# Half-unit operand places, reordered cosine steps and six sum places in a fused attention and two-MLP kernel

## The chip, the cores and the metric

The kernel runs on one core of one Trainium2 chip, in one launch. The metric is the device time of that launch in microseconds. The core's engines are named as in the profile: PE multiplies matrices (PEld is its weight load), DVE is the vector engine, ACT the scalar engine, POOL the third elementwise engine, and SP is the queue that issues every DMA of this kernel.

## The reference

Attention over mean-pooled keys, then two MLPs over the 4608 x 512 result, all in float32:

```python
x = attention(q, k pooled by 8, v pooled by 8)        # (4608, 512)
gate = sigmoid(x @ w_gate)                            # w_gate, w_val: (512, 1536)
x = (gate * (x @ w_val)) @ w_out                      # w_out: (1536, 512)
h = x @ w_in                                          # w_in: (512, 2048)
out = (h * cos(h)) @ w_out2                           # w_out2: (2048, 512)
```

## The kernel before, in words

Every matrix operand is held as two float32r parts, a high part (a rounded copy, made by ACT) and a low part (what is left of it, made by DVE in `split_lo`, line 65); three matmuls, high by high, high by low and low by high, make one product. The large products use a seven-product scheme on quarter blocks (as Strassen's), so sums of blocks are made on POOL. All intermediate results go through DRAM. Tokens are taken in nine chunks of 512; `GROUPS` are chunk 0 alone and four pairs of chunks.

The launch runs in four stages, each ending before the next begins on PE:

- **Gate and value** (`gv_step`, `gated`): attention, `w_gate` and `w_val` for all chunks. The gated results go to DRAM (`od`).
- **Units of `w_out`** (line 817 on): for each of the four pairs, seven products of three units each, 84 units. A unit is 12 matmuls of 128x512, 6 for each of its two halves. `unit_fetch` (848) loads a unit of 512 KB from `od` into one of three raw places `uf`; `unit_high` (841) makes the high part with one ACT cast of 128x1024 into one of two `up` places; `unit_low` (836) makes the low part with one DVE subtraction. A `up` place can be written again only when PE has finished the unit in it. `unit_go` (860) does one such step of each kind and is called about once per unit, so casts are issued at most two units ahead of the matmuls. When a product is done (`product_done`, 924), its two PSUM banks are copied by ACT (line 930) or added by DVE (line 940) into one of the `ok` tiles in pool `hm`, which has five places `x0` to `x4`; POOL makes sums of these tiles (`x_sum`, line 910), and SP stores them to `xd` (line 907). Between units the same engines prepare `w_in`: SP loads 16 raw blocks of 512 KB (`i2_begin`, 274), ACT and DVE convert them, and `i2_fill` (322) splits 28 weights. What happens at which unit is written by hand: `at_(n, f)` (898) puts `f` at the n-th following call of `due` (901), which is called once per unit.
- **Cosine blocks** (`Block`, `h_block`, line 1055): h and h cos h for five groups of eight blocks. A block has seven products of 6 matmuls each, in the order 0, 3, (product 6 of the block before), 2, 1, 5, 4, in PSUM banks A to D, of which there are two sets. `kept` (1007) copies a bank, `whole` (1011) rounds to an integer on ACT, `rest` (1015) takes the fraction on DVE, `sine` (1022) is on ACT and `times` (1026) on DVE; line 1061 copies bank A to C, lines 1080 and 1088 add a bank to a kept tile. POOL makes four sums per block (1042). `after(pos)` follows each product and calls `due`; operands `x` of the next group are loaded (955), cast (960) and split (65) from there. In group 0 matmuls have 256 columns, in groups 1 to 4 they have 512.
- **Second output product** (`y_chunk`): operands `sp` come back from DRAM (1141), are cast (1152) and split, and 28 weights `wy` of 512 KB take the places of the weights of the cosine stage during its last group.

Within an engine all instructions run in the order in which the program issues them; there is no scheduler.

Of the kernel before, what the change touches and what calls it, by code (L numbers as in the profile page):

```python
# [9 lines left out]
F32 = mybir.dt.float32  # L10
# [12 lines left out]
def attention_two_mlps(  # L23
# [794 lines left out]
    count = {"fetched": 0, "high": 0, "low": 0, "done": 0, "go": 0}  # L818
    o_weights, o_tags, o_raw, o_parts = [], [], {}, {}
# [13 lines left out]
    uf = []  # L833
    issued = {}

    def unit_low():
        x, raw = o_parts[count["low"]], o_raw.pop(count["low"])
        split_lo(nc.vector, x[:, 1], raw, x[:, 0])
        count["low"] += 1

    def unit_high():
        k = count["high"]
        x = xq.tile([P, 2, 2, C], F32R, tag=f"q{3 + k % 2}", name=f"up{k}")
        nc.scalar.copy(x[:, 0], o_raw[k])  # L844
        o_parts[k] = x
        count["high"] += 1

    def unit_fetch():
        k = count["fetched"]
        g, n, m = units[k]  # L850
        pool, tag = uf[k % 3]
        t = pool.tile([P, 2, C], F32, tag=tag, name=f"uf{k}")
        nc.sync.dma_start(
            t.rearrange("p m (i n) -> p m i n", i=2), od[g][O_PRODUCTS[n][1], :, 2 * m:2 * m + 2]
        )
        o_raw[k] = t
        issued[k] = count["go"]
        count["fetched"] += 1

    def unit_go():  # L860

        if count["low"] < count["high"]:
            unit_low()
        count["go"] += 1
        if count["high"] < min(count["done"] + 2, count["fetched"]):
            if count["go"] - issued[count["high"]] >= 2:
                unit_high()
        if count["fetched"] < min(count["low"] + len(uf), len(units)):
            unit_fetch()

    def unit_step():

        k = count["done"]
        g, n, m2 = units[k]
        while count["low"] <= k:
            unit_go()
        which, fresh = O_PRODUCTS[n][2:]
        if n < 2 and m2 == 0:
            po[g, which] = [bank("tg"[g % 2 == 0], [P, C], f"po{g}_{which}{u}") for u in range(2)]
        w = o_weights[k % PER]  # L880
        x = o_parts.pop(k)
        for m in range(2):
            first, final = fresh and m2 == 0 and m == 0, m2 == STEPS - 1 and m == 1
# [7 lines left out]
        if m2 == STEPS - 1:  # L891
            product_done(g, n, po[g, which])
# [663 lines left out]
```

## Time and profile before

| quantity | value |
|---|---|
| time, median of 3 runs | 1885.22 us (1883.74 to 1885.65) |
| the profiled execution | 1891.42 us, its span 1889.7 us |
| busy PE, DVE, ACT, POOL | 1753.8, 1103.1, 896.3, 629.7 us |
| DMA | 401.77 MB, mean 213 GB/s |
| gate and value, units of `w_out` | 0 to 778.6 us, 778.6 to 1124.8 us |
| cosine blocks, second output product | 1124.8 to 1529.3 us, 1529.3 to 1889.7 us |

The stage bounds are the first matmuls of lines 887, 991 and 1229 (lines 626 to 628 and 789 to 791 come before). Busy PE counts overlapping matmuls by modelled ends, so within a stage its gaps say more than its sum.

### The profile page before, as it was taken

The numbers are of one execution on the slowest core, as the hardware profiler recorded it, in microseconds if no ns is written. First come the engines' busy times: TensorE is split into PE (matmuls) and PEld (weight loads), VectorE is DVE, ScalarE is ACT, GpSimd is POOL, SyncE is SP. The second block draws the span as 40 slices with busy tenths as digits, with TensorE's granted clock in tenths as the row PEclk, the third lists the DMA queues.
The fourth block names the chain that finished last, engine by engine and source line by source line (L and its number), as shares of the span: only waits on it lengthen the run. The fifth ranks groups of instructions, "written<-read, shape, count | busy, mean of one in ns | idle before, by whom it ended". The sixth has DMA issues, their size and how long they took to land. (4 is left out here: it accounts for less than half of the span.)

```text
span 1889.7 us, 26169 instructions
## 1 busy us (share of the span) xinstructions
PE 1753.8 (93%) x9360; PEld 1430.4 (76%) x9360; DVE 1103.1 (58%) x1734; ACT 896.3 (47%) x1513; POOL 629.7 (33%) x622
## 2 busy tenths in 40 slices
PE   7999999999999999886778768999999989999999
PEld 5887888888888888665556557777777778888887
DVE  7956565475654621264535555676767666655565
ACT  7555445354544521243434435565666544444443
POOL 2314546345453332223322024465656430000000
PEclk8999999999999999997989989999999999999999
DMA  9635757657666479576556635485768997676663
GB/s 274 183 101 159 212 167 238 190 173 210 217 206 223 154 274 307 191 251 213 187 182 204 213 142 173 157 266 174 245 195 265 343 345 260 224 228 205 224 202 127
DMA packets 266418, 401.77 MB, mean 213 GB/s; under 512 B 54448, under 2 KB 197808, under 8 KB 266288
## 3 DMA queue, kind: packets, MB, share of 16 engines
q1 hardware_dynamic: 266288, 400.10, 65.6%
q8 instruction: 73, 1.20, 0.3%
q14 instruction: 57, 0.47, 0.1%
HBM read 226.75 MB, written 173.28 MB: 212 GB/s over the span
## 5 line engine op out<-in xcount | busy, mean ns | idle before, releaser
L640 DVE TENSOR_TENSOR g<-pv,g 128x512 f32<-128x512 f32 (+1 forms) x111 | 74.9, 675 | 299.0 <-issue 148.4
L65 DVE TENSOR_TENSOR sp<-sp,sp 128x1024 fp32r<-128x1024 f32 x126 | 154.0, 1262 | 97.5 <-ACT sp L1152 97.4
L626 PE MATMUL pg<-xT,wg 128*128 128x512 f32 (+1 forms) x444 | 179.3, 404 | 3.9 <-ACT e L551 3.0
L628 PE MATMUL pg<-xT,wg 128*128 128x512 f32 (+1 forms) x444 | 172.5, 389 | 2.2 <-DVE wg L65 2.2
L627 PE MATMUL pg<-xT,wg 128*128 128x512 f32 (+1 forms) x444 | 172.2, 388 | 0.8 <-DVE xT L65 0.8
L626 PE MATMUL pv<-xT,wv 128*128 128x512 f32 (+1 forms) x444 | 170.9, 385 | 2.1 <-DVE g L640 2.1
L628 PE MATMUL pv<-xT,wv 128*128 128x512 f32 (+1 forms) x444 | 170.9, 385 | 0.0
L627 PE MATMUL pv<-xT,wv 128*128 128x512 f32 (+1 forms) x444 | 170.8, 385 | 0.0
L65 DVE TENSOR_TENSOR up<-uf,up 128x1024 fp32r<-128x1024 f32 x84 | 119.5, 1434 | 75.3 <-ACT up L844 75.0
L844 ACT CAST up<-uf 128x1024 fp32r<-128x1024 f32 x84 | 88.1, 1050 | 150.4 <-PE po_A L889 66.4
L1042 POOL TENSOR_TENSOR s_S<-z_a,z_a 128x512 f32<-128x512 f32 (+1 forms) x80 | 100.3, 1276 | 170.7 <-DVE z_a L1026 170.7
L991 PE MATMUL pha<-x,hw 128*128 128x512 f32 (+1 forms) x320 | 129.1, 403 | 24.3 <-DVE ph L1088 13.4
L639 ACT ACTIVATE g<-pg 128x512 f32<-128x512 f32 (+1 forms) x111 | 65.0, 587 | 153.6 <-PE pg L628 92.5
L1229 PE MATMUL py_A<-wy,sp 128*128 128x512 f32 x432 | 135.7, 395 | 0.0
L1152 ACT CAST sp<-sp 128x1024 fp32r<-128x1024 f32 x126 | 124.3, 1058 | 12.5 <-DMA sp<-sd 12.5
L995 PE MATMUL pha<-x,hw 128*128 128x512 f32 (+1 forms) x320 | 120.2, 376 | 0.0
L996 PE MATMUL pha<-x,hw 128*128 128x512 f32 (+1 forms) x320 | 120.1, 375 | 0.0
L888 PE MATMUL po_A<-up,so 128*128 128x512 f32 x192 | 83.5, 435 | 37.5 <-DVE up L65 37.5
L1022 ACT ACTIVATE z_a<-z_a 128x512 f32<-128x512 f32 (+1 forms) x160 | 93.8, 587 | 45.3 <-DVE z_a L1015 45.3
L991 PEld LDWEIGHTS pha<-x,hw 128*128 128x128 f32 x320 | 61.2, 191 | 60.8 <-DVE ph L1088 24.7
L628 PEld LDWEIGHTS pg<-xT,wg 128*128 128x128 f32 x444 | 84.4, 190 | 20.1 <-DVE wg L65 2.4
L626 PEld LDWEIGHTS pg<-xT,wg 128*128 128x128 f32 x444 | 84.7, 191 | 19.6 <-ACT e L551 3.2
(193 smaller groups left out, 4449.1 us busy)
## 6 DMA issues: line engine op xcount, KB each, us to landing
sp<-sd SPq DMA_DIRECT2D x126, 512.0 KB
uf<-od SPq DMA_DIRECT2D x84, 512.0 KB
sd<-s_S SPq DMA_DIRECT2D x128, 256.0 KB
od<-tg SPq DMA_DIRECT2D x48, 512.0 KB
sd<-z_a SPq DMA_DIRECT2D x96, 256.0 KB
wo<-wo SPq DMA_DIRECT2D x40, 512.0 KB
raw_o<-in_moe_w_out_dram SPq DMA_DIRECT2D x28, 512.0 KB
x<-xd SPq DMA_DIRECT2D x28, 512.0 KB
```

Of the source, the lines that this page charges most:

```text
L65: engine.tensor_tensor(out=lo, in0=x, in1=hi.bitcast(F32), op=ALU.subtract)
L626: nc.tensor.matmul(p, wh, x[:, 0, kb], start=kb == 0, stop=False)
L627: nc.tensor.matmul(p, wh, x[:, 1, kb], start=False, stop=False)
L628: nc.tensor.matmul(p, wl, x[:, 0, kb], start=False, stop=kb == KB - 1)
L844: nc.scalar.copy(x[:, 0], o_raw[k])
L991: nc.tensor.matmul(p, wh, x[:, 0, kb], start=k in (0, 3) and kb == 0, stop=False, skip_group_check=True,)
L995: nc.tensor.matmul(p, wh, x[:, 1, kb], start=False, stop=False, skip_group_check=True)
L996: nc.tensor.matmul(p, wl, x[:, 0, kb], start=False, stop=kb == 1, skip_group_check=True)
L1022: nc.scalar.activation(z, z, AF.Sin, scale=TURN)
L1042: nc.gpsimd.tensor_tensor(out=z[name], in0=z[x], in1=z[y], op=op)
L1152: nc.scalar.copy(hi[:, r], lo[:, r].bitcast(F32))
L1229: nc.tensor.matmul(p, x[0][:, m, s], w, start=fresh and m == 0, stop=False, skip_group_check=True,)
```

## The change

Three things are rewritten.

1. **Units of `w_out` become 168 halves** of 6 matmuls each. There are four tiles of two places each, eight places, allocated once (`up`). A half of 256 KB is loaded straight into the low part of its place, ACT casts it into the high part, and DVE subtracts in place. The raw places `uf` are gone. After the matmuls of half v the program issues the split of half v+3, the cast of half v+4 and the load of half v+8. The first eight loads, six casts and four splits are issued in the last steps of the stage before.
2. **Sums get six places** (`a` to `f`), and a table `HOMES` says which result of which pair goes where; three stores of sums are issued one unit earlier. The `w_in` raw blocks use other places, and `i2_fill` of the last pair comes one unit earlier.
3. **Cosine steps are issued in another order** within a block, directly and not through `at_`: the previous block's last steps (`a`) stand between the present block's (`b`). Casts of `x` are all on ACT, and POOL splits one operand of a group where it split three. The first operands and the weights of the last stage are issued from a table of positions (`put`), the first operand's split in two parts in two blocks.

```diff
-    def unit_high():
-        k = count["high"]
-        x = xq.tile([P, 2, 2, C], F32R, tag=f"q{3 + k % 2}", name=f"up{k}")
-        nc.scalar.copy(x[:, 0], o_raw[k])
...
+    def up_of(v):
+        return up[v // 2 % len(up)][:, v % 2]
+
+    def half_fetch(upto):
+        while count["fetched"] < min(upto + 1, len(halves_of)):
+            v = count["fetched"]
+            g, n, m = halves_of[v]
+            nc.sync.dma_start(
+                up_of(v)[:, 1].bitcast(F32).rearrange("p (i n) -> p i n", i=2),
+                od[g][O_PRODUCTS[n][1], :, m],
+            )
+            count["fetched"] += 1
...
+    def half_step(v):
...
+        half_low(v + 3)
+        half_high(v + 4)
+        half_fetch(v + 2 * len(up))
+        if final:
             product_done(g, n, po[g, which])
...
+    HOMES = {
+        (1, 0): "a", (1, 1): "e", (1, 2): "c", (1, "S2"): "d", (1, 6): "b",
+        (2, 0): "e", (2, 1): "c", (2, 2): "a", (2, "S2"): "b", (2, 6): "d",
+        (3, 0): "c", (3, 1): "a", (3, 2): "e", (3, "S2"): "d", (3, 6): "f",
+        (4, 0): "a", (4, 1): "e", (4, 2): "b", (4, "S2"): "c", (4, 6): "d",
+    }
...
-            t = hm.tile([P, 2, C], F32, tag=f"x{n if n < 6 else 3}", name=f"ok{g}_{n}")
-            o_keep[n] = t
+            t = o_keep[n] = home(g, n)
...
+        if b:
+            b.product(5)
+        if a:
+            a.sums()
+        if b:
+            b.sine("a11")
+            nc.vector.tensor_tensor(out=b.p["B"], in0=b.p["B"], in1=b.z["a12"], op=ALU.add)
+            b.times("a11", "C")
+            b.whole("a12", "B")
         after(5)
-        step(4)
-        nc.vector.tensor_tensor(out=b.p["D"], in0=b.p["A"], in1=b.z["a22"], op=ALU.add)
-        b.whole("a22", "D")
-        at_(1, lambda: b.rest("a22", "D"))
-        at_(1, lambda: b.sine("a22"))
-        at_(2, lambda: b.times("a22", "D"))
-        at_(3, lambda: b.store("a22"))
+        if b:
+            b.product(4)
+            nc.vector.tensor_tensor(out=b.p["D"], in0=b.p["A"], in1=b.z["a22"], op=ALU.add)
+            b.rest("a12", "B")
+            b.whole("a22", "D")
+            b.store("a11")
         after(6)
...
-        for k in range(len(units)):
-            unit_step()
-            unit_go()
-            due()
+        for v in range(len(halves_of)):
+            half_step(v)
+            if v % 2:
+                due()
...
-            high = nc.vector if j in (4, 6) else None
-            low = nc.gpsimd if j in (1, 3, 5) else nc.vector
...
+                engine = nc.gpsimd if j == 4 else nc.vector
```

In the rows below, `ok` are the sum tiles, `po` PSUM banks of `w_out`, `up` its operands, `hw` and `raw_i` weights of `w_in`, `pha` and `phb` banks A and B, `ph` banks C and D, `z` the tiles of a block (a11 to a22 its quarters).

On ACT, around the copy of pair 2's first product, one row before is a cast of a whole unit:

```order
L844 CAST up24_8187<-uf24_8143 128x1024
L148 ACTIVATE raw_i23_8096<-raw_i23_8096 128x512 x2
L930 COPY ok2_0_8206<-po2_A0_8149 128x512
L930 COPY ok2_0_8206<-po2_A1_8150 128x512
L844 CAST up25_8210<-uf25_8166 128x1024
```

and now two rows of halves stand ahead of the copy, of the places q3 and q4:

```order
L854 CAST up_q3_7024<-up_q3_7024 128x512 x2
L148 ACTIVATE raw_i23_8124<-raw_i23_8124 128x512 x2
L854 CAST up_q4_7025<-up_q4_7025 128x512 x2
L932 COPY ok2_0_8245<-po2_A0_8180 128x512
L932 COPY ok2_0_8245<-po2_A1_8181 128x512
```

One more unit (24 and 25, as halves) is cast before the copy that waits for PE.

On ACT in the cosine stage, block 3 of group 2, before:

```order
L1011 ACTIVATE z2_3_a11_11146<-ph3_9501 128x512
L1011 ACTIVATE z2_3_a12_11136<-phb1_9505 128x512
L1022 ACTIVATE z2_3_a11_11146<-z2_3_a11_11146 128x512
L1011 ACTIVATE z2_3_a22_11114<-ph1_9499 128x512
L1022 ACTIVATE z2_3_a12_11136<-z2_3_a12_11136 128x512
L1061 COPY ph2_9500<-pha0_9502 128x512
```

and now:

```order
L1013 ACTIVATE z2_3_a11_11237<-ph3_9597 128x512
L1024 ACTIVATE z2_3_a11_11237<-z2_3_a11_11237 128x512
L1013 ACTIVATE z2_3_a12_11225<-phb1_9601 128x512
L1013 ACTIVATE z2_3_a22_11203<-ph1_9595 128x512
L1052 COPY ph2_9596<-pha0_9598 128x512
L1024 ACTIVATE z2_3_a12_11225<-z2_3_a12_11225 128x512
```

The sine of a11 now stands ahead of the rounding of a12, and the next block's bank copy ahead of the sine of a12. On DVE the order of `times` of a11, lines 1080 and 1088 is the same as before; the two fractions of a12 and a22 now stand before the two `times`.

## Rows read from the trace of the kernel before

**Rows 1.** Windows: stretch, length, busy of five engines (count), granted clock, DMA share, GB/s.

```profile
700.00:778.60 78.60, 78.43 (x347) 64.60 (x346) 13.17 (x20) 12.17 (x21) 16.27 (x21) 1.00 0.80 271
778.60:1124.80 346.20, 265.91 (x1009) 201.36 (x1010) 182.44 (x178) 139.06 (x183) 88.59 (x54) 0.90 0.60 198
1124.80:1187.90 63.10, 49.97 (x338) 44.56 (x337) 32.48 (x79) 35.21 (x93) 27.34 (x30) 0.95 0.60 186
1187.90:1270.80 82.90, 81.39 (x347) 63.20 (x346) 57.47 (x88) 51.59 (x93) 45.93 (x36) 1.00 0.63 202
...
1438.80:1529.30 90.50, 80.76 (x328) 62.18 (x327) 60.08 (x86) 51.72 (x92) 48.01 (x35) 0.96 0.93 317
```

**Rows 2.** Waits, 778.6 to 1124.8: us in total, times, longest us.

```profile
ACT up L844 <- PE po_A L889: 66.4, 27, 7.4
...
PE po_A L888 <- DVE up L65: 37.5, 25, 5.8
...
ACT ok L930 <- DMA xd<-ok: 30.3, 3, 12.5
...
PE po_B L887 <- ACT up L844: 22.9, 3, 10.1
```

**Rows 3.** Timeline of PE after one gap: start, us, instruction, [idle before].

```profile
1052.01 0.80 PE L887 MATMUL po_B<-up,so 128*128 128x512 f32 x1 [6.38 <-ACT up L844]
...
1055.44 0.63 PE L887 MATMUL po_B<-up,so 128*128 128x512 f32 x1
1055.87 0.63 PE L888 MATMUL po_B<-up,so 128*128 128x512 f32 x1
...
1057.55 0.39 PE L889 MATMUL po_B<-up,so 128*128 128x512 f32 x1
...
1058.92 0.39 PE L889 MATMUL po_B<-up,so 128*128 128x512 f32 x1
```

**Rows 4.** Groups by line, 778.6 to 1124.8: busy us, mean ns, idle before.

```profile
L65 DVE TENSOR_TENSOR up<-uf,up 128x1024 fp32r<-128x1024 f32 x84 | 119.5, 1434 | 75.3 <-ACT up L844 75.0
L844 ACT CAST up<-uf 128x1024 fp32r<-128x1024 f32 x83 | 87.0, 1050 | 149.3 <-PE po_A L889 66.4 <-PE po_B L889 56.7 <-DMA uf<-od 16.1
...
L65 DVE TENSOR_TENSOR hw<-raw_i,hw 128x512 fp32r<-128x512 f32 (+1 forms) x30 | 22.0, 743 | 60.6 <-ACT hw L322 60.6
...
L65 DVE TENSOR_TENSOR x<-x 128x512 fp32r<-128x512 f32 x7 | 7.0, 994 | 0.0
```

**Rows 5.** Timelines of SP and ACT: a unit's load issued, its cast starting.

```profile
783.88 1.49 SPq L853 DMA_DIRECT2D uf<-od  x2
...
788.57 1.04 ACT L844 CAST up<-uf 128x1024 fp32r<-128x1024 f32 x1 [8.81 <-DMA uf<-od]
```

**Rows 6.** Timelines of ACT and DVE in one block of group 1.

```profile
1220.02 0.58 ACT L1061 COPY ph<-pha 128x512 f32<-128x512 f32 x1
...
1226.48 0.60 ACT L1011 ACTIVATE z_a<-phb 128x512 int32<-128x512 f32 x1 [1.54 <-DVE phb L1080]
...
1230.09 0.58 ACT L1061 COPY ph<-pha 128x512 f32<-128x512 f32 x1
...
1227.63 0.69 DVE L1026 SCALAR_TENSOR_TENSOR z_a<-z_a,ph 128x512 f32<-128x512 f32 x1 [1.24 <-ACT z_a L1022]
1228.24 0.69 DVE L1088 TENSOR_TENSOR ph<-pha,z_a 128x512 f32<-128x512 f32 x1
```

**Rows 7.** Waits, 1124.8 to 1529.3, same columns as rows 2.

```profile
PEld pha L991 <- DVE ph L1088: 24.7, 37, 4.9
...
ACT z_a L1007 <- DMA xd<-ok: 6.4, 1, 6.4
```

**Rows 8.** Windows of 8 us in the last cosine group, columns as rows 1.

```profile
1457.00:1465.00 8.00, 7.92 (x35) 6.00 (x34) 5.09 (x9) 4.44 (x9) 5.10 (x4) 1.00 1.00 335
...
1489.00:1497.00 8.00, 3.49 (x13) 2.60 (x12) 6.18 (x6) 3.90 (x7) 4.26 (x3) 0.84 1.02 348
```

**Rows 9.** Tile view of `up`: ns min/median/max, first and last start.

```profile
L65 DVE TENSOR_TENSOR up<-uf,up x84: 1210/1224/3369, 779.1 to 1117.3; 128x1024 fp32r<-128x1024 f32 x84
```

More of the change, by code (lines that the diff above doesn't have):

```diff
@@ L817, in attention_two_mlps @@
     PER = len(O_PRODUCTS) * STEPS
-    count = {"fetched": 0, "high": 0, "low": 0, "done": 0, "go": 0}
-    o_weights, o_tags, o_raw, o_parts = [], [], {}, {}
+    halves_of = [
+        (g, n, m) for g in range(1, len(GROUPS)) for n in range(len(O_PRODUCTS)) for m in range(HF)
+    ]
+    count = {"fetched": 0, "high": 0, "low": 0}
+    o_weights, o_tags, up = [], [], []
     def so_load(tag):
@@ L890, in unit_step @@
-        count["done"] += 1
-        if m2 == STEPS - 1:
+        w = o_weights[STEPS * n + m // 2][:, m % 2]
+        x = up_of(v)
+        first, final = fresh and m == 0, m == HF - 1
+        for u in range(2):
+            wh, wl = (w[:, i, u * P:(u + 1) * P] for i in range(2))
+            p = po[g, which][u]
+            nc.tensor.matmul(p, wh, x[:, 0], start=first, stop=False, skip_group_check=True)
+            nc.tensor.matmul(p, wh, x[:, 1], start=False, stop=False, skip_group_check=True)
+            nc.tensor.matmul(p, wl, x[:, 0], start=False, stop=final, skip_group_check=True)
@@ new lines, in sums, with h_block @@
+                at_(2 + n + n // 2, lambda name=name: self.store(name))
+    def h_block(b, a, after):
+        if b:
+            b.product(0)
+            nc.scalar.copy(b.p["C"], b.p["A"])
+        if a:
+            a.sine("a12")
+            a.rest("a22", "D")
+        after(0)
+        if b:
+            b.product(3)
+            b.kept("a22", "B")
+        if a:
+            a.sine("a22")
+            a.times("a12", "B")
+        after(1)
+        if a:
+            a.product(6)
+            a.whole("a21", "A")
+            a.times("a22", "D")
+            a.rest("a21", "A")
+            a.store("a12")
+        after(2)
+        if b:
+            b.product(2)
+            b.kept("a12", "A")
+        if a:
+            a.sine("a21")
+            a.times("a21", "A")
+            a.store("a22")
+        after(3)
+        if b:
+            b.product(1)
+            b.whole("a11", "C")
+            b.rest("a11", "C")
+        after(4)
+        if b:
+            b.product(5)
+        if a:
+            a.sums()
+        if b:
+            b.sine("a11")
+            nc.vector.tensor_tensor(out=b.p["B"], in0=b.p["B"], in1=b.z["a12"], op=ALU.add)
+            b.times("a11", "C")
+            b.whole("a12", "B")
+        after(5)
+        if b:
+            b.product(4)
[3 more added lines that the diff above has]
+            b.store("a11")
@@ L1501, in attention_two_mlps @@
+        put(final, PAIRS, 3, lambda: y_fetch(3))
+        put(final, PAIRS, 6, lambda: y_fetch(4))
+        y_count["split"] = 2
+        y_ring.extend(ring[(7 * final + n) % len(ring)] for n in range(len(ring)))
+        def after(g, m, pos):
+            for fn in spot.pop((g, m, pos), ()):
+                fn()
+            due()
         before = None
@@ L1506, in attention_two_mlps @@
                 before = b
-        before.last()
-        due()
-        due()
-        y_split(1)
+        h_block(None, before, lambda pos: after(len(GROUPS), 0, pos))
         while events:
             due()
-        y_fetch(4)
-        y_slots.extend(h_tags[24:])
-        load_last()
-        assert not y_todo
+        assert not y_todo and not spot
         hp_.release()
```

224 lines of the change are left out of this document (88 added, 136 removed).

## The prediction

> **What bounds the kernel now.** I read the windows by stage first, then the waits and the timeline of the stage that stood out, then one block of the cosine stage.
>
> In the windows [rows 1] the stretch before the units ends with PE busy 78.43 of 78.60 us. The unit stage, 346.2 us, has PE busy for 265.9, so 80.3 us are gaps, and its granted clock is 0.90. What the stage would take without either is read from the timeline of PE [rows 3]: from 1057.55 to 1058.92 six matmuls of 128x512 start in 1.37 us, 0.2283 us each, so its 1008 matmuls need 230.2 us. The stage loses 116.0 us: the 80.3 of gaps, and 35.7 in which PE runs slowly. The same timeline shows that these belong together: after a gap of 6.38 us the matmuls start 0.43 us apart (1055.44, 1055.87), the lower of the two clock levels (1.2 and 2.4 GHz), and at 1057.55 the higher one is back.
>
> Who makes the gaps is in the waits [rows 2]. PE waits 37.5 us for DVE's low parts and 22.9 for ACT's high parts in the two largest groups. ACT itself waits 66.4 us for PE, because one of the two operand places must be empty before the next unit is cast, and then 30.3 us in only three waits, up to 12.5 us each, until the store of a sum tile has been read out, so that the tile can be written again. Everything behind that copy on ACT, the next casts among it, stands still, and PE then starves. No engine is full: DVE is busy 182.4 us, ACT 139.1, POOL 88.6, DMA 0.60 of the time [rows 1]. The stage is bound by how few units are prepared ahead, not by any engine's work.
>
> The cosine stage is near PE's floor. A block of 512 columns takes 10.07 us (the bank copies at 1220.02 and 1230.09, [rows 6]); its 42 matmuls need 42 x 0.2283 = 9.59. Inside the block ACT waits 1.54 us for the sum of line 1080 before it rounds a12, makes the sine of a11 only then, DVE waits 1.24 us for that sine, and only then comes line 1088, on which PE's weight load waits 24.7 us in all [rows 6, 7].
>
> **The change part by part, units.** ACT gets 168 casts of half size for 84: between half of 1.050 us [rows 4] and the 0.60 of another ACT instruction of 128x512 [rows 6]; I take 0.59, nearest in shape, 99 us, and ACT's 139 become 150 of 230. DVE gets 168 splits between half of 1.434 us and the 0.743 of the weights' splits [rows 4]; by 0.743, 125 us for 119.5, and 182 become 188 of 230. SP issues 84 loads more; the bound is 0.75 us each (1.49 for two, [rows 5]), 168 x 0.75 = 126 of 230 us. All of this lies beside PE, if the cover holds.
>
> The cover: a half takes PE 6 x 0.2283 = 1.37 us. The load of half v+8 is issued when PE is through with half v, and PE wants it seven halves later, after 9.6 us. A load of a whole unit landed 4.7 us after its issue (783.88 to 788.57, [rows 5]); with cast and split 4.7 + 0.59 + 0.74 = 6.0 us, and 3.6 are to spare. ACT no longer waits for PE before a cast, but only for data. The sum tiles' 30.3 us go, since each of the six places is written again only two products or more after its last store was issued: PE takes 8.2 us per product, and the longest wait for a store was 12.5. A cast or split behind a bank copy that waits for PE has three to four halves, 4 to 5.5 us, of lead.
>
> What is late next: in the last pair DVE does 42 splits (0.72), 21 weights (0.743), 7 operands (0.994, [rows 4]) and 6 bank sums of 0.69 (the price of line 1088, [rows 6]): 30.2 + 15.6 + 7.0 + 4.1 = 56.9 of the pair's 57.5 us. With no room there I estimate 6 us of gaps. Each other pair sends seven stores of 512 KB within about twenty halves beside the loads, 3 us each by estimate, 9. At the start the ninth load stands behind the last stores of the stage before, which held SP until 783.88 [rows 5], about 3.9 us after PE is through with the first half: 2 us after the spare time. Together 17, so the stage takes 247 us, **99 less**. DMA carries the same 346.2 x 198 = 68.5 MB, now 277 GB/s; 271 at a share of 0.80 and 317 at 0.93 [rows 1] scale to about 340, so it is four fifths full. The ends: 230 us (116 less), and, if only the 271 GB/s were to be had, 253 + 17 = 270 (76 less).
>
> The Trainium skill (DMA: Bandwidth & Descriptors, Rules for kernel authors) speaks against halving transfers: it asks for 1 MiB per DMA and for small ones to be joined. In the last cosine group stores of 256 KB and loads of 512 KB together moved 335 and 348 GB/s at a share of 1.00 to 1.02 [rows 8], so the row shows no loss from transfers of that size; by the skill's fixed 2 us for each (Anatomy of one DMA), 84 more would be an estimated 168 us if nothing overlapped, and the sum 1925.
>
> **Cosine stage.** Group 0 takes 63.1 us with PE busy for 50.0 [rows 1]. Of the gaps, the first kept tile's 6.4 us wait for a sum tile's store [rows 7] goes, since that memory now belongs to a tile that was stored a pair earlier. In the new order line 1088 waits for neither the rounding of a12 nor the sine behind it; a cast (1.05) and a split per block remain in the chain. I take 52 us, **11 less** (ends 13 and 0).
>
> Groups 1 to 3 take 250.9 us (1187.9 to 1438.8); 24 x 9.59 = 230.2. What is late next is the cast and split of the next group's operands, now on ACT and DVE almost alone: 3.3 us per change of group by estimate, two or three casts of 1.05. So 240 us, **11 less** (ends 21 less and, should these queue worse, 5 more).
>
> Group 4 takes 90.5 us. Its hole, PE busy 3.49 of 8 us from 1489 [rows 8], is the first output operand's cast and split, now spread over two blocks. Eight blocks of 9.59 are 76.7, but the DMA share there is 0.93 at 317 GB/s [rows 1]: 28.7 MB at 340 take 84 us. I take 84, **7 less** (ends 14 and 0), because nothing in the change lessens these bytes. The output product itself is left as it is.
>
> The sum is 99 + 11 + 11 + 7 = 128 us. The profiled execution took 1891.4, which gives 1763; the median shown is 6.2 us lower, so I predict **1757**.
>
> **Rivals.** *DVE becomes the bound of the unit stage.* Its splits range from 1.210 to 3.369 us [rows 9], with a mean of 1.434 [rows 4], so something holds them at times; POOL is busy for 88.6 us of the stage. If every microsecond of POOL's work held DVE, 188 + 89 = 277 us would be the stage: 69 less, with the cosine stage's 29 less 98, 1787. Against it: the mean lies only 0.22 above the shortest, 19 us over 84 splits.
>
> The Trainium skill (SBUF — State Buffer, Who interferes with whom) has this as a rule: a DVE instruction with two SBUF inputs and a GpSimd instruction that reads SBUF shut each other out, for the whole instruction. The spread of the splits agrees.
>
> *The cosine order gives nothing:* roundings of a22 and the copy to C now wait on ACT behind line 1088, and what that loses equals what is won. Then only the units' 99 remain, 1786. For it: ACT and DVE hand over to each other some twelve times in a block, and PE is only 0.48 us per block above its floor.
>
> *Slower: loads land too late for eight places.* The old pace is 346.2 / 168 = 2.06 us per half. Eight places give the same pace when a round takes 16.5 us, that is when a half lands 16.5 - 1.37 - 0.59 - 0.74 = 13.8 us after its issue; from about 15 on the cosine gain is eaten too. At 16 the stage takes 168 x 18.7 / 8 = 393 us, 47 more, and the run 1757 + 99 + 47 = 1903. For it: one store was waited for 12.5 us [rows 2], and loads stand on SP behind stores that wait for POOL. Against it: 4.7 us for twice the size.
>
> *The change does not do what it says:* should the two halves of a tile only come free together, there are four places of a unit, a round of 4.7 + 1.05 + 1.43 + 2.74 = 9.9 us, 2.5 per unit, still under PE's 2.74. That would cost only spare time, some 10 us, and lies in the forecast's range.
>
> **How the numbers follow.** Forecast 0.70, DVE bound 0.14, cosine order without gain 0.12, late loads 0.04. All best ends together give 1721 and all worst 1814; the range 1722 to 1800 holds the forecast's spread and the two milder rivals, and leaves out late loads and the far tails. About 0.2% (3.8 us) is what a measurement of this kernel can tell from no change; only late loads of about 15 us come there. So faster 0.96, same 0.01, slower 0.03.
>
> **What would show it.** Right: the unit stage ends near 1026 us with clock 0.97 or more, ACT has no wait of its bank copies for stores, group 0 takes about 52 us, and bank copies of plain blocks are 9.6 us apart. Wrong: PE's waits for DVE above 20 us in the unit stage (DVE bound), casts waiting for loads by more than 20 us (late loads), blocks still 10.07 apart, or a new wait at the start of the output product, where the faster group 4 leaves DMA more to catch up.

## The result and the profile after

The changed kernel takes **1763.04 us** (median of 4 runs, 1761.68 to 1763.56) against 1885.43 us (4 runs, 1883.74 to 1885.76) beside it: a ratio of 0.9351, 95% interval 0.9335 to 0.9368. The forecast was 1757 us, with a range of 1722 to 1800. The profiled execution took 1761.68 us, its span is 1759.9 us, the granted clock 0.988 (0.971 before).

The windows by stage of the kernel after, with the columns of [rows 1]: units, cosine group 0, groups 1 to 3, group 4, output product.

```profile
777.00:1022.80 245.80, 236.12 (x1010) 190.15 (x1009) 204.22 (x261) 147.63 (x262) 87.45 (x54) 0.99 0.84 279
1022.80:1072.40 49.60, 43.34 (x333) 40.82 (x332) 35.27 (x78) 34.58 (x92) 27.45 (x27) 1.00 0.66 202
1072.40:1308.00 235.60, 232.29 (x1020) 189.89 (x1018) 180.80 (x260) 165.03 (x285) 140.97 (x101) 1.00 0.70 227
1308.00:1386.60 78.60, 76.18 (x332) 61.77 (x332) 59.20 (x86) 54.78 (x94) 42.03 (x31) 1.00 0.97 337
1386.60:1759.90 373.30, 355.35 (x2017) 308.80 (x2015) 211.49 (x254) 154.81 (x200) 10.25 (x8) 0.98 0.67 221
```

Read against the same stages before, every stage up to the fourth is shorter and the last one is longer:

| stage | before | forecast | after | change |
|---|---|---|---|---|
| units | 346.2 | 247 | 245.8 | -100.4 |
| cosine group 0 | 63.1 | 52 | 49.6 | -13.5 |
| groups 1 to 3 | 250.9 | 240 | 235.6 | -15.3 |
| group 4 | 90.5 | 84 | 78.6 | -11.9 |
| output product | 360.4 | 360.4 | 373.3 | **+12.9** |

With 1.6 us at the start these make the 129.8 us between the two spans.

In the unit stage the waits (776 to 1023 us, columns of [rows 2]) have turned round. ACT's casts wait for data; for PE they wait 11.9 us, where the two groups before made 123.1 [rows 4], and no bank copy waits for a store:

```profile
PE po_A L877 <- DVE up_q L65: 3.6, 3, 3.1
PE po_A L877 <- DVE up_u L65: 3.2, 3, 2.6
...
ACT up_q L854 <- DMA up_q<-od: 43.7, 29, 8.7
```

PE's waits in the stage are 9.6 us over all groups, where the two largest alone were 37.5 and 22.9 [rows 2]. The 43.7 us that ACT spends waiting for loads cost PE little; the experiments below show how little room is left.

In the cosine stage the weight load's wait of 24.7 us [rows 7] has become 9.3, and the bank copies of two plain blocks of group 1, in ACT's timeline, stand 9.52 us apart (10.07 in [rows 6]). The blocks that also cast operands of the next group stand up to 11.0 apart, so the mean over groups 1 to 3 is 9.82 (10.45 before):

```profile
1092.15 0.57 ACT L1052 COPY ph<-pha 128x512 f32<-128x512 f32 x1
...
1101.67 0.57 ACT L1052 COPY ph<-pha 128x512 f32<-128x512 f32 x1
```

What was lost again is in the first products of the output product. First PE, then ACT, POOL and SP of the kernel after, around 1400 us:

```profile
1408.38 1.22 PE L1240 MATMUL py_A<-wy,sp 128*128 128x512 f32 x2 [10.51 <-ACT sp L1154]
```

```profile
1389.95 1.05 ACT L1154 CAST sp<-sp 128x1024 fp32r<-128x1024 f32 x1 [4.32 <-DMA sp<-sd]
...
1406.31 1.07 ACT L1178 COPY m<-py_A 128x512 f32<-128x512 f32 x2 [9.94 <-POOL s_S L1044]
1407.27 2.00 ACT L1154 CAST sp<-sp 128x1024 fp32r<-128x1024 f32 x2
```

```profile
1402.24 1.26 POOL L1044 TENSOR_TENSOR s_S<-z_a,z_a 128x512 f32<-128x512 f32 x1 [3.19 <-DMA sd<-s_S]
1403.67 1.26 POOL L1044 TENSOR_TENSOR s_S<-s_S,z_a 128x512 f32<-128x512 f32 x1 [0.17 <-DMA sd<-s_S]
1405.01 1.26 POOL L1044 TENSOR_TENSOR s_S<-z_a,s_S 128x512 f32<-128x512 f32 x1
```

```profile
1391.26 0.96 SPq L1147 DMA_DIRECT2D sp<-sd  x2
...
1397.72 4.84 SPq L1122 DMA_DIRECT2D wy<-td  x4
...
1403.60 0.93 SPq L1147 DMA_DIRECT2D sp<-sd  x2
```

PE stands 10.51 us for the cast of operand 2. That cast (1407.27) stands on ACT behind the copy of product 0's banks, and the copy waits 9.94 us for POOL: it begins at 1406.31, when POOL's last sum ends (1405.01 + 1.26). The tile `m1` that the copy writes was placed by the program's memory plan at the address of a12 of the last cosine block, and S4 = a12 - S2 is the last of POOL's four sums to read it. (The trace shows the wait and not the address; moving the tile, below, tests it.) POOL itself waits for the stores that must empty its six `s` tiles, and from 1330 to 1418 us DMA is full (a share of 1.04 to 1.08 in each window of 8 us). Before, the same copy waited 2.56 us for POOL and PE 2.5 us in two waits; now PE waits 10.5 and 2.8. The rest of the 12.9 goes with the clock behind the gap:

```profile
1402.00:1410.00 8.00, 1.58 (x3) 0.86 (x4) 1.64 (x2) 2.96 (x4) 3.79 (x3) 0.52 1.04 404
1410.00:1418.00 8.00, 6.84 (x32) 5.58 (x31) 2.34 (x4) 2.10 (x2) 0.00 (x0) 0.84 1.06 404
```

Two things meet here, an address and a full DMA; which of them decides was the first question.

### The profile page after: what moved, and what is told of

It reads as the page before. It is cut to its first block, busy times and chain, and to the rows that moved or that the text cites. A ratio compares the mean times of both kernels' runs of the same rounds, so it can differ in the third digit from the quotient of the medians.

```text
span 1759.9 us, 26862 instructions
## 1 busy us (share of the span) xinstructions
PE 1702.6 (97%) x9360; PEld 1419.0 (81%) x9360; DVE 1127.7 (64%) x1818; ACT 917.8 (52%) x1605; POOL 614.6 (35%) x614
## 4 chain that ended last, share of the span: by engine, by line
PE 52%; DMA 4%; DVE 2%; ACT 1%; issue 1%; POOL 0%; DVEq 0%; SPq 0%; ACTq 0%; POOLq 0%
PE py_A L1240 7%; PE py_B L1240 4%; PE pha L993 4%; PE py_A L1245 4%; PE pha L997 3%; PE pha L998 3%; PE po_A L877 2%; PE py_B L1245 2%; PE po_A L878 2%; PE po_A L876 2%; PE py_C L1240 2%; PE phb L993 2%; PE phb L997 2%; PE phb L998 2%; PE po_B L877 2%; PE po_B L876 1%
## 5 line engine op out<-in xcount | busy, mean ns | idle before, releaser
L65 DVE TENSOR_TENSOR sp<-sp,sp 128x1024 fp32r<-128x1024 f32 x126 | 149.1, 1224 | 105.6 <-ACT sp L1154 105.6
L1044 POOL TENSOR_TENSOR s_S<-z_a,z_a 128x512 f32<-128x512 f32 (+1 forms) x80 | 115.4, 1464 | 149.0 <-DVE z_a L1028 118.7
L1240 PE MATMUL py_A<-wy,sp 128*128 128x512 f32 x432 | 137.1, 399 | 10.5 <-ACT sp L1154 10.5
L993 PE MATMUL pha<-x,hw 128*128 128x512 f32 (+1 forms) x320 | 120.6, 377 | 8.3 <-DVE ph L1096 6.8
L997 PE MATMUL pha<-x,hw 128*128 128x512 f32 (+1 forms) x320 | 118.1, 369 | 3.7 <-DVE x L65 3.7
L65 DVE TENSOR_TENSOR up_q<-up_q 128x512 fp32r<-128x512 f32 x126 | 107.7, 890 | 21.7 <-ACT up_q L854 21.6
L998 PE MATMUL pha<-x,hw 128*128 128x512 f32 (+1 forms) x320 | 117.8, 368 | 0.0
L854 ACT CAST up_q<-up_q 128x512 fp32r<-128x512 f32 x126 | 75.7, 622 | 58.3 <-DMA up_q<-od 43.7
L626 PEld LDWEIGHTS pv<-xT,wv 128*128 128x128 f32 x444 | 84.7, 191 | 19.1 <-DVE g L640 2.6
L1245 PEld LDWEIGHTS py_A<-wy,sp 128*128 128x128 f32 x432 | 81.8, 190 | 20.1 <-DVE sp L65 0.8
```

Source lines behind the costliest of these rows:

```text
L65: engine.tensor_tensor(out=lo, in0=x, in1=hi.bitcast(F32), op=ALU.subtract)
L626: nc.tensor.matmul(p, wh, x[:, 0, kb], start=kb == 0, stop=False)
L993: nc.tensor.matmul(p, wh, x[:, 0, kb], start=k in (0, 3) and kb == 0, stop=False, skip_group_check=True,)
L997: nc.tensor.matmul(p, wh, x[:, 1, kb], start=False, stop=False, skip_group_check=True)
L998: nc.tensor.matmul(p, wl, x[:, 0, kb], start=False, stop=kb == 1, skip_group_check=True)
L1044: nc.gpsimd.tensor_tensor(out=z[name], in0=z[x], in1=z[y], op=op)
```

## The experiments

Two theories of the lost 12.9 us: **place** (the copy lies where the last sums still read) and **bytes** (DMA has too much to carry, whatever waits for it). For the gains: do the parts add up, and are **depth** (how far ahead halves are loaded), the **six sum places** and the **one pair of steps** on ACT what the prediction says they are?

### Each half of the change alone

`units_alone` is the changed kernel with the `Block`, `h_block` and position code of the kernel before; `cosine_alone` is the kernel before with that code of the changed one.

> The changed kernel with the cosine stage (order of the steps, fetches of operands, start of the output product) of the kernel before. If the parts add up as the two traces place them, the unit stage stays at 246 us (-100.4) and the groups of the cosine stage return to 251 and 90 us: 1885.4 - 100.4 = 1785 us; down to 1779 if the 6.4 us that the first kept tile waited for a store belong to the new places of the sum tiles and not to the cosine order. The wait of PE for the second operand at the start of the output product should be under 3 us here. Rival: the stages feed each other (a unit stage that ends 100 us earlier leaves the stores of its sums to the cosine stage): then the cosine stage takes longer than before and the time is over 1792.

> The kernel before with the cosine stage of the changed kernel. If the parts add up: -13.6 in group 0, -15.2 in groups 1 to 3, -11.9 in group 4, +12.9 at the start of the output product, together -27.8: 1885.4 - 27.8 = 1857.6 us; 1864 if the 6.4 us of group 0 belong to the places of the sum tiles. The wait of PE py_A for ACT's cast at the start of the output product (10.5 us) should be here too, at 8 us or more, because nothing of the units is left in memory there. Rival: that wait comes from the units' side (transfers that were pushed back): then it is under 3 us here, and the time is near 1846.

| | units | group 0 | groups 1 to 3 | last 7 copies | output product | median |
|---|---|---|---|---|---|---|
| before | 345.9 | 63.2 | 250.9 | 78.4 | 355.9 | 1885.4 |
| units alone | 245.6 | 56.6 | 250.6 | 78.7 | 358.3 | 1784.9 |
| cosine alone | 340.3 | 57.7 | 238.1 | 67.2 | 370.6 | 1870.2 |
| after | 245.6 | 49.7 | 235.7 | 66.7 | 368.4 | 1763.0 |

(All in us; units to the start of their last matmul, groups from bank copy to bank copy, the output product to the start of its last matmul.) Units alone come to 1784.9 us, ratio 0.9457 (0.9440 to 0.9474): as forecast, and without the new wait, since PE's longest wait in the output product is 2.4 us. Group 0 falls by 6.6 us here too, so half of its gain belongs to this half of the change: ACT's wait of 7.0 us for a sum tile's store, ahead of the first kept tile, is still there in the trace of cosine alone and gone in this one. Cosine alone gives 1870.2, ratio 0.9907 (0.9889 to 0.9925), 6 us more than the upper expectation: the order wins 29 us up to the last block, not 34, and the output product gives 14.7 of them back, PE's wait for operand 2 (9.2 us) among it. So the loss comes with the cosine order and needs nothing of the units. The unit stage of cosine alone, whose code is that of before, is 5.6 us shorter in its trace, so a gain of some 100 us that is read from one trace of before is known to about 6. The two halves make 102 and 17 us against their runs of before, 119 together; the change makes 122.

### How far ahead the halves must be loaded

```diff
-  for pool, tag in ((xq, "q3"), (xq, "q4"), (xq, "q6"), (ufp, "u"))
+  for pool, tag in ((xq, "q3"), (xq, "q4"), (xq, "q6"))
```

With four places, casts and splits are issued one half later too:

```diff
-  for pool, tag in ((xq, "q3"), (xq, "q4"), (xq, "q6"), (ufp, "u"))
+  for pool, tag in ((xq, "q3"), (xq, "q4"))
-        half_low(v + 3)
-        half_high(v + 4)
+        half_low(v + 2)
+        half_high(v + 3)
```

The loads of the run-up are cut to the same number. With four places two casts of the run-up come before their halves are loaded, so the first values are not the reference's; the work is the same.

> The changed kernel with three operand tiles in place of four, six halves: a load is issued five halves before PE wants it (6.9 us), not seven (9.6). The prediction's cover: 4.7 us of landing, 0.59 of cast, 0.74 of split are 6.0 us, so 0.9 us are to spare where 3.6 were; plain stretches hold, the bursts of stores cost more. Unit stage 252 to 265 us (246 with eight places), time 1770 to 1782. Rival, depth does not matter beyond a few places (the gain is that casts wait for data and not for PE): stage 246 to 250, time 1763 to 1767.

> The changed kernel with two operand tiles, four halves, and with cast and split one half closer to their use (three and two halves ahead). The prediction's round: 4.7 + 0.59 + 0.74 + 1.37 = 7.4 us for four places, 1.85 us per half, 168 x 1.85 = 311 us for the unit stage, 65 more: time 1828; with the longer landing in the bursts of stores up to 1850. Rival, depth does not matter: under 1775.

The windows of the unit stage, with six places and with four:

```profile
777.30:1051.90 274.60, 246.03 (x1010) 193.65 (x1009) 194.84 (x261) 149.85 (x263) 81.92 (x54) 0.96 0.77 252
```

```profile
776.50:1113.50 337.00, 269.08 (x1009) 197.47 (x1008) 194.91 (x261) 148.33 (x263) 81.34 (x54) 0.93 0.64 204
```

Six places cost 28.8 us in the stage (1789.9 us in all, ratio 0.9490, 0.9456 to 0.9524), four cost 91 (1856.3, 0.9842, 0.9805 to 0.9878). Depth is the cause: with four places three quarters of what the whole change won is gone, though the halves, the loads into place and the free ACT are still there. Whether the same depth in whole units, four of them loaded in place, would have done as well was not tried.

Both cost more than the cover of the prediction allowed. One half of the changed kernel, in the timelines of SP, ACT, DVE and PE, shows where the time goes: load, cast, split, and the first matmul that reads the low part.

```profile
811.88 0.32 SPq L844 DMA_DIRECT2D up_u<-od  x1
816.62 0.62 ACT L854 CAST up_u<-up_u 128x512 fp32r<-128x512 f32 x1
819.46 0.68 DVE L65 TENSOR_TENSOR up_u<-up_u 128x512 fp32r<-128x512 f32 x1
821.66 0.39 PE L877 MATMUL po_B<-up_u,so 128*128 128x512 f32 x1
```

Over all halves of the changed kernel, each load paired with its cast, split and matmul in this way, the means are 5.0 us from issue to cast, 3.3 from there to the end of the split, and 1.8 to spare. The prediction had 4.7, 1.3 and 3.6. So the load was about right and the way through ACT and DVE was not: a split starts 1.8 us after the end of its cast, in the mean, where the prediction let it follow at once. The spare time is a mean too; 14 halves have under 0.15 us of it. With six places the three means are 4.2, 2.6 and 1.5, with four 3.6, 2.4 and 0.7, and 24 and 64 halves have under 0.15 us to spare.

### The six places of the sums undone

```diff
     HOMES = {
-        (1, 0): "a", (1, 1): "e", (1, 2): "c", (1, "S2"): "d", (1, 6): "b",
...
+        (g, n): tag for g in range(1, len(GROUPS))
+        for n, tag in ((0, "a"), (1, "b"), (2, "c"), (6, "d"), ("S2", "e"))
     }
```

> The changed kernel with five places for the sum tiles and the assignment of the kernel before (each product always in the same place). Theory: three bank copies a run wait again for a store to be read out, 30.3 us in all (up to 12.5 each), and casts stand behind them; PE has 4 to 5.5 us of prepared halves, so 15 to 20 us of the 30 show in the unit stage, and 6.5 in group 0 of the cosine stage (its first kept tile): time 1784 to 1792. Rival: the eight places cover these waits, then 1763 to 1770.

The first sum tile of the start also goes to place `e`. ACT's waits in the unit stage:

```profile
ACT ok L930 <- DMA xd<-ok: 13.2, 3, 4.4
```

Three bank copies wait for a store again, but 13.2 us and not 30.3, and the stage takes 250.2 us, 4.4 more. Seven runs with the unit code of the changed kernel, itself among them, lie between 245.0 and 248.7 us (to the start of the last matmul; 250.0 here), so that is little. PE waits 3.0 us at the first kept tile of group 0. The time is 1769.9 us (two runs), ratio 0.9384 (0.9348 to 0.9420), an interval that touches the changed kernel's. The expectation (1784 to 1792) falls, and its rival (1763 to 1770) came out: eight operand places cover most of such a wait. The stores also go out earlier here than in the kernel before, because three of them are still issued one unit earlier. The six places are worth some 7 us by the medians, not 20.

### One pair of steps put back

```diff
-            b.sine("a11")
             nc.vector.tensor_tensor(out=b.p["B"], in0=b.p["B"], in1=b.z["a12"], op=ALU.add)
-            b.times("a11", "C")
             b.whole("a12", "B")
+            b.sine("a11")
+            b.times("a11", "C")
```

> The changed kernel, with the sine of a11 and its product put behind the sum of the bank and the rounding of a12 again, on ACT and DVE, as the kernel before has them; all else of the new order stays. Theory of the prediction: this order set the block's pace, so plain blocks go back from 9.52 to 9.9 to 10.07 us, groups 1 to 3 from 235.7 to 246 to 250 and group 4 by 3 to 4: time 1776 to 1782. Rival: the gain came from spreading the last steps of a block over the next block, and this pair alone costs nothing: blocks at most 9.6 apart, time under 1767.

The waits of PEld over the cosine stage of this run, and of ACT over its groups 1 to 3:

```profile
PEld pha L993 <- DVE ph L1096: 34.6, 22, 2.4
```

```profile
ACT z_a L1013 <- DVE phb L1089: 49.2, 24, 3.4
```

1791.3 us, ratio 0.9500 (0.9475 to 0.9524): 28 us lost by two instructions of ACT that stand in the other order (DVE's order is the same), more than expected. Groups 1 to 3 take 255.0 us, longer than the 250.9 of the kernel before. ACT stands at the rounding of a12 until DVE has summed bank B (49.2 us here, 24.2 in the changed kernel), the sine of a11 waits behind it, DVE waits for that sine, and the sum into bank D (line 1096) on which the weight load waits comes last.

But the loss is not in every block. Bank copies of group 1 in ACT's timeline:

```profile
1100.02 0.59 ACT L1052 COPY ph<-pha 128x512 f32<-128x512 f32 x1
1109.53 0.59 ACT L1052 COPY ph<-pha 128x512 f32<-128x512 f32 x1
1119.05 0.59 ACT L1052 COPY ph<-pha 128x512 f32<-128x512 f32 x1
1130.10 0.59 ACT L1052 COPY ph<-pha 128x512 f32<-128x512 f32 x1
1141.10 0.59 ACT L1052 COPY ph<-pha 128x512 f32<-128x512 f32 x1
```

A block without a cast stays at 9.51 us with the pair put back, where 9.9 to 10.07 were expected. From the block on in which ACT casts the first operand of the next group (1123.99), copies stand 11.0 us apart, where the changed kernel has 9.65 to 10.8. So both theories hold in part: this chain limits the blocks that also cast operands, and the 0.55 us that a block without them gained on the kernel before belong to the rest of the new order. Which of its steps gives them was not tried.

### Place or bytes

`sums_elsewhere` allocates the tiles of the output product once, in an order that puts the first two kept banks on tiles of the last block but one. `early_operand` issues the load of operand 1 one block earlier:

```diff
+            if s == 1:
+                x.reverse()
-        put(final, PAIRS - 1, 1, lambda: y_fetch(1))
+        put(final, PAIRS - 2, 1, lambda: y_fetch(1))
```

> The changed kernel, with the tiles of the output product's kept banks and sums at other addresses: the first two lie on tiles of the last block but one. Theory of the place: ACT's first kept copy waited 9.94 us because its tile lies on a12 of the last block, which POOL reads last of all, and the second operand's cast stands behind that copy. Then the copy's wait goes to under 1 us, PE's wait of 10.5 us falls to the one for operand 2 (its load was issued at 1391.3; 7 to 9 us of landing, then cast and split): 2 to 4 us, and the time is about 1756. Rival, bytes: DMA is full until 1418 us, so what is only placed elsewhere wins nothing; PE's wait stays at 9 to 11 us, now for the operand's load, and the time is 1761 to 1764.

> The changed kernel, with the second operand of the output product (product 1) loaded one block earlier, into the one of its two places that is free by then. Theory of the order: ACT stood 4.32 us before the cast of that operand, with the last block's sines behind it, so the last block's sums on POOL end some 4 us earlier, and PE's 10.5 us become about 6.5: time near 1759. Rival, bytes: 1 MB that is moved forward pushes the stores of the same blocks back by some 2.8 us (at 370 GB/s), POOL waits for those, and nothing is won: 1762 to 1764.

ACT's and PE's timelines with the tiles elsewhere:

```profile
1396.44 1.06 ACT L1178 COPY t_m<-py_A 128x512 f32<-128x512 f32 x2
1399.45 1.04 ACT L1155 CAST sp<-sp 128x1024 fp32r<-128x1024 f32 x1 [1.95 <-DMA sp<-sd]
```

```profile
1400.55 0.73 PE L1237 MATMUL py_A<-wy,sp 128*128 128x512 f32 x2 [2.69 <-ACT sp L1155]
...
1412.52 1.22 PE L1237 MATMUL py_B<-wy,sp 128*128 128x512 f32 x2 [3.75 <-ACT sp L1155]
```

The copy comes 9.9 us earlier, although POOL's last sum ends no earlier (1407.0 us, 1406.3 in the changed kernel), and PE's wait for operand 2 is 2.69; for operand 3 it is now 3.75. The time is 1757.0 us, ratio 0.9307 (0.9291 to 0.9324), clear of the changed kernel's interval. With the load of operand 1 earlier, ACT and POOL show:

```profile
1410.97 1.07 ACT L1180 COPY m<-py_A 128x512 f32<-128x512 f32 x2 [14.96 <-POOL s_S L1044]
```

```profile
1409.67 1.26 POOL L1044 TENSOR_TENSOR s_S<-z_a,s_S 128x512 f32<-128x512 f32 x1
```

ACT's 4.32 us before the cast of operand 1 are gone, ACT then waits 14.96 us for POOL, and PE 10.6: 1764.7 us, ratio 0.9346 (0.9327 to 0.9365), no gain. So bytes make POOL late, and moving a load among them helps nobody; the address makes PE pay 10.5 us for it, and 2.69 are left with the tiles elsewhere.

`fewer_bytes2` leaves out 16 stores of the last group:

> The changed kernel without 16 of the 32 stores of the four sums in the last cosine group (blocks 3 to 6, 256 KB each, 4.2 MB, some 11 us of a full DMA); the output product of the last pair of chunks reads the operands of the pair before it instead, so its output is not the reference's. Place and order are those of the changed kernel. If late stores are what makes POOL late, and POOL the copy: POOL's waits for stores (22.2 us) nearly go, its last four sums end 5 us behind DVE's last step, near 1402, ACT's copy waits 4 to 5 us and PE 5 to 6 in place of 10.5: time 1755 to 1759. If the place alone decided, whatever DMA carries: PE's wait stays at 9 us or more and the time at 1761 to 1764.

It ran 1753.4 us (0.9291, 0.9274 to 0.9308), but does not separate the two as meant: with the stores gone, the memory plan put a12 of the last block elsewhere, so that place and bytes changed together; ACT's copy began at 1391.52 after a wait of 0.28 us, while POOL's last sum ended at 1399.1. What it does show is the next such address, in DVE's timeline:

```profile
1407.86 0.42 DVE L1170 SCALAR_TENSOR_TENSOR y<-m 128x256 f32<-128x256 f32 x1 [9.34 <-DMA sd<-s_S]
```

DVE waits 9.34 us to write a sum of the output, which lies on an `s` tile whose store is late, the split of operand 3 stands behind it, and PE waits 7.4 us, with 4.2 MB less to carry.

### Order and place together

On top of `sums_elsewhere` the loads of operands 3 and 4 go ahead of the last weights:

```diff
-            put(final, m, 9, weights)
+            put(final, m, 12 if m >= PAIRS - 2 else 9, weights)
-        put(final, PAIRS, 3, lambda: y_fetch(3))
-        put(final, PAIRS, 6, lambda: y_fetch(4))
+        put(final, PAIRS, 0, lambda: y_fetch(3))
+        put(final, PAIRS, 3, lambda: y_fetch(4))
```

> The changed kernel with the tiles of the output product's kept banks and sums elsewhere, and with the loads of operands 3 and 4 of the output product issued ahead of the last seven loads of its weights (needed only from product 4 on). Theory: with the place mended, PE waited 2.7 us for operand 2 and 3.8 for operand 3, because these loads stood on SP behind weights; both go to under 3 us together, and the low clock behind them (two windows of 8 us at 0.79 and 0.64) costs some 4 us less: time 1744 to 1753 us. Rival, bytes: DMA is full until 1426 us whatever the order, so the wait moves to the weights of product 4 or to another kept bank, and the time stays at 1755 to 1759.

1754.0 us, ratio 0.9287 (0.9269 to 0.9305). Whether this order gains on `sums_elsewhere` stays open, for the intervals overlap. PE's wait of 3.75 us for operand 3 is 0.75 now, and a wait of 2.28 us has come at product 4, where ACT's copy of another kept bank waits for a store:

```profile
1418.16 1.07 ACT L1178 COPY t_m<-py_A 128x512 f32<-128x512 f32 x2 [5.66 <-DMA sd<-s_S]
```

To the start of its last matmul the output product takes 368.4 us in the changed kernel, 363.9 with the tiles elsewhere, 360.3 with the order too, and 355.9 before (one trace each). So the place is worth 4.5 us of the 12.5 lost, the order another 3.6, and 4.4 stay.

### POOL's sums and DVE's splits

The splits of the changed kernel take 0.89 us each (busy time by count), not 0.743. DVE's and POOL's timelines in one stretch of the unit stage show why:

```profile
844.30 1.35 DVE L65 TENSOR_TENSOR up_u<-up_u 128x512 fp32r<-128x512 f32 x1
845.57 1.35 DVE L65 TENSOR_TENSOR hw<-raw_i,hw 128x512 fp32r<-128x512 f32 x1
846.85 1.35 DVE L65 TENSOR_TENSOR up_u<-up_u 128x512 fp32r<-128x512 f32 x1
848.12 1.28 DVE L65 TENSOR_TENSOR up_q<-up_q 128x512 fp32r<-128x512 f32 x2
```

```profile
842.52 5.13 POOL L300 TENSOR_TENSOR raw_i<-raw_i 128x256 f32<-128x256 f32 x4
```

While POOL runs four instructions of 1.28 us (842.5 to 847.7), each split starts 1.27 us after the one before; at 848.12, POOL idle, two take 1.28 together. The bank sums of line 942, one of whose inputs lies in PSUM, keep 0.68 us in the same stage. This is the rule of the Trainium skill that the prediction quoted (SBUF — State Buffer, Who interferes with whom), and the trace agrees. `fewer_pool` leaves out three of the four large sums that POOL makes of each pair (S2 stays):

```diff
-        x_sum(a21, a11, a21, ALU.subtract)
+        if g == 0:
+            x_sum(a21, a11, a21, ALU.subtract)
         x_sum(s2, a22, a21, ALU.subtract)
-        x_sum(a11, a11, s2, ALU.add)
+        if g == 0:
+            x_sum(a11, a11, s2, ALU.add)
...
-        x_sum(a12, a12, s2, ALU.subtract)
+        if g == 0:
+            x_sum(a12, a12, s2, ALU.subtract)
```

> The changed kernel without 12 of the 15 large sums on POOL in the unit stage (of each pair S1, S3 and S4; S2 stays, all stores stay), so what the sums feed is not the reference's. POOL's busy time in the stage falls by some 31 of 87 us. If a running POOL sum holds DVE's splits (684 ns in the median, but up to 2892, and 890 in the mean): the mean of the 168 splits falls to about 810, the longest to under 1.6 us, and PE's 9.6 us of waits to 3 to 6: time 1755 to 1761. If the long splits have another cause: mean and longest stay, time 1762 to 1764.

Groups of the splits in the unit stage, first of the changed kernel, then of this one:

```profile
L65 DVE TENSOR_TENSOR up_q<-up_q 128x512 fp32r<-128x512 f32 x124 | 106.4, 893 | 21.7 <-ACT up_q L854 21.6
L65 DVE TENSOR_TENSOR up_u<-up_u 128x512 fp32r<-128x512 f32 x42 | 41.7, 1005 | 2.4 <-ACT up_u L854 2.4
```

```profile
L65 DVE TENSOR_TENSOR up_q<-up_q 128x512 fp32r<-128x512 f32 x124 | 98.2, 824 | 32.3 <-ACT up_q L854 32.0
L65 DVE TENSOR_TENSOR up_u<-up_u 128x512 fp32r<-128x512 f32 x42 | 36.2, 873 | 4.9 <-ACT up_u L854 4.9
```

Over these rows a split takes (98.2 + 36.2) / 166 = 0.81 us, as expected, and (106.4 + 41.7) / 166 = 0.89 in the changed kernel; the longest is still 2.9, beside the S2 sums that stay. The unit stage takes 235.9 us, 9.9 less and within 6 of its floor; the time is 1754.4 us (0.9297, 0.9279 to 0.9315). All stores are still there, but they no longer wait for POOL on SP, so how much of the 9.9 us is held splits and how much is loads that stood behind such stores stays open.

`sums_on_dve`, the last run, has two edits on top of `order_and_place`: the first two sums of each pair are made by DVE, and the kept banks of products 2 and 3 lie on other tiles.

```diff
-        x_sum(a21, a11, a21, ALU.subtract)
-        x_sum(s2, a22, a21, ALU.subtract)
+        engine = nc.vector if g else nc.gpsimd
+        engine.tensor_tensor(out=a21, in0=a11, in1=a21, op=ALU.subtract)
+        engine.tensor_tensor(out=s2, in0=a22, in1=a21, op=ALU.subtract)
```

> The last kernel (order and place mended) with two edits in two stages. In the unit stage the first two of three sums of each pair (8 sums of 128x1024) go from POOL to DVE. If a running POOL sum holds DVE, DVE gives 8 x 1.22 = 9.8 us (the price of a DVE subtraction of 128x1024) and gets back some 8 x 1.3 = 10 us of held splits: its busy time stays within 5 us of 204, no split next to these sums takes 2.9 us, and since the sums are done sooner PE waits less: stage 240 to 246 us. Rival, POOL's sums cost DVE nothing: DVE's busy time rises by 10 us or more and the stage goes to 248 to 256. At the start of the output product the last kept banks move off the tiles of the last sums: ACT's copy waited 5.66 us there for a store and PE 2.3 us behind it; expected under 1 us. Time 1746 to 1752 by the theory, 1755 to 1764 by the rival.

Its unit stage:

```profile
775.90:1018.90 243.00, 234.62 (x1008) 190.51 (x1007) 193.68 (x269) 147.99 (x262) 65.56 (x46) 0.99 0.83 279
```

DVE takes over eight sums (1.22 us each, 9.8 in all), and its busy time *falls* from 204.2 to 193.7 us (204.5 in `order_and_place`): by this sum it had lost some 20 us to being held beside these eight. The stage is 2.8 us shorter than the changed kernel's, and 2 us shorter than the shortest of the seven with the same unit code. In the output product ACT's waits for stores are gone, but PE waits 4.11 us at product 5 for an operand that ACT had to wait for:

```profile
1417.61 0.99 PE L1238 MATMUL py_B<-wyb,sp 128*128 128x512 f32 x2 [4.11 <-ACT sp L1156]
```

There the bytes do decide. The kernel takes **1748.6 us**, ratio 0.9269 (0.9256 to 0.9281): 14 us less than the changed kernel, the lowest median of all; against `order_and_place` the intervals overlap.

## Why the prediction was right, point by point

- **What bounds the unit stage** ("by how few units are prepared ahead, not by any engine's work"): shown. Four places bring back most of the old time with the engines no busier than with eight (DVE 194.9 us, ACT 148.3 of 337).
- **The units' term** (-99, measured -100.4): right in sum, not in its parts. The 17 us above the floor are 15.6; they were split into 6 of a full DVE, 9 of store bursts and 2 at the start. Without most of POOL's sums and with all stores about 10 of them vanish, so POOL is behind more than half. The price of a split was mis-sized (0.743 taken, 0.89 measured), and so was the cover: cast and split take 3.3 us of a half's way and not 1.3, so 1.8 us are to spare where the text saw 3.6.
- **The sum tiles' stores**: the 30.3 us go, as said, but most of them would have been covered by the eight places; the six places are worth some 7 us.
- **Cosine stage**: the gain came, 2.5 us larger (group 0) and 4.3 (groups 1 to 3) than the terms; the mechanism is shown only in part. The prediction put the pace of every block down to line 1088 behind the rounding of a12 and the sine. The one pair put back shows this for the blocks that also cast operands; the others keep 9.51 to 9.52 us with the pair put back, so their step from 10.07 has another cause in the new order, which stays open. The floor of 9.59 was a little high, for plain blocks take 9.52, and a change of group, put at 3.3 us, came to (235.6 - 24 x 9.52) / 3 = 2.4.
- **Group 4** (-7, because "nothing in the change lessens these bytes"): mis-sized. It took 78.6 us, not 84; its bytes were not a floor for the stage, since what was not yet stored could slide into the next one, where DMA stays full until 1418. In the 78.6 us it moved 26.5 MB (at 337 GB/s), not the 28.7 of before.
- **"The output product itself is left as it is"**: this is the step that failed, by 12.9 us, twice the miss of the whole forecast. It was true of the instructions and not of the stage's start. The sentence that named what would show it wrong had the place and the full DMA; it lacked the third link, that a tile of the next stage lies on an address that the last sums still read. What the other stages won beyond their terms (1.4, 2.5, 4.3 and 4.9, together 13.1) hides it in the total.
- **The total**: the sum gave 1763 us against the profiled execution, and that took 1761.7. The 6 us between 1757 and the median come from the last step: the profiled execution lay 6.2 us above the median before, and lies 1.4 below it after.
- **Rivals**: DVE did not become the bound, though its splits are held as that rival says; late loads did not come, though the sign named for them did: casts waited 50.7 us for loads (43.7 and 7.0), where more than 20 was to speak for it. PE's own waits, 9.6 us in all, were the better sign, since a cast that waits costs nothing while prepared halves last. Six places in place of eight would have begun that rival; the cosine order gave its gain. The two halves of a tile do come free one at a time: of even and odd halves alike, the load that follows is issued 0.2 us before the modelled end of the half that it replaces (median).
- **Against halving transfers** (the Trainium skill, DMA: Bandwidth & Descriptors, Rules for kernel authors): the unit stage moved 279 GB/s with its loads in 256 KB and 289 without most of POOL's sums, so no loss from the size shows here. The sum of 1925 us by the fixed 2 us did not come near; the section that the prediction names gives that figure for DMAs that GpSimd issues, and here SP issues all of them. What smaller loads do need is more of them under way, as the runs with six and four places show.

## What to carry to other kernels

When a stage ends sooner, read the start of the next one as if it were new: which transfers slide into it, and which of its first tiles lie on addresses that the stage before still reads or stores; an engine that waits for such a tile holds everything behind it. In a pipeline count the places that an operand needs from the issue of its load to its last use, with the landing time under load and with the time that it stands in the queues of the engines between, and give one more. On an engine that runs strictly in order, an instruction whose input comes late belongs behind those whose inputs are there: one swapped pair on ACT was worth 28 us over 40 blocks, though nothing in those blocks of groups 1 to 3 that cast no operands.

## What was not expected of the hardware

A DVE subtraction of two SBUF tiles of 128x512 took 0.67 to 0.69 us in all 112 splits of the changed kernel that met no POOL instruction. Beside POOL instructions of 128x256 the splits took up to 1.35 us, beside those of 128x1024 up to 2.89. So a sum of 128x1024 on POOL (2.6 us) can cost DVE more than making it itself (1.22 us): eight sums moved to DVE lowered its busy time by 10.5 us. And the time from the issue of a 256 KB load to its cast, where the cast stood idle for it, grew with the traffic of the stage: medians of 3.0 us with four places at 204 GB/s, 3.6 with six at 252, 4.2 with eight at 279, and at the longest 8.4, although the transfers are half as large as the one that took 4.7 [rows 5].
